# The last two chunks of a local attention and MoE kernel as one pair: GEMM1 with seven block products for eight

## The chip, the core and the metric

The kernel runs on one core of one Trainium2 chip. The metric is the device time of one execution in microseconds (us). A core has TensorE (PE, the matmuls), VectorE (DVE), ScalarE (ACT), GpSimd (POOL) and SyncE (SP, which issues the DMAs); they run side by side and wait for each other by semaphores. PE writes to eight PSUM banks of 128 x 512 floats; DVE and ACT read them.

## The reference

Attention makes x (4608 tokens x 512); a gated two-layer network follows, and it fills most of the time:

```python
out_up  = softmax attention on q, k, v averaged over 4 rows, repeated 4 times
out_local = softmax attention within |i - j| < 4
x = (out_up + out_local).transpose(0, 2, 1, 3).reshape(4608, 512)

def _moe_ref(x, w_in, w_out):          # w_in 512 x 2048, w_out 2048 x 512
    h = x @ w_in                       # GEMM1
    relu6 = np.clip(h + 3.0, 0.0, 6.0)
    g = h * relu6 / 6.0
    return (g @ w_out)                 # GEMM2
```

## The kernel before

**Precision.** Every operand of the two GEMMs is held as two fp32r parts: the rounded value (high) and what it leaves out (low). A product is three matmuls: high x high, high x low, low x high. For W_in these parts are the tiles `win[f]` (128 x 2 x 512; f is one of 16 blocks of 128 hidden columns, named wp in the trace), for W_out `wout[f]`; both stay in SBUF from the first chunk on.

**Chunks.** The 4608 tokens are nine chunks of 512 (0 to 8). For a chunk `plan_split` (line 958) makes the parts of x in the one buffer `rounded` (ACT or DVE the high part, L120 or L122; DVE or POOL the low part, L969), which is free when the chunk before has been through GEMM1. `plan_moe` (line 1050) then does for each f: `gemm1` (L1067), 12 matmuls into PSUM bank h0 or h1 (4 slices of 128 rows of W_in x 3 terms); `relu` on ACT (L1073); `gate` on DVE (L1077), which frees the bank; `hi` on ACT (L1081) and `lo` on DVE or POOL (L1085), the parts of g. `gemm2` (L1125) adds 12 matmuls per f into four banks o0 to o3, four groups of 128 tokens with 3 each. After the last f `plan_store` evicts each of the four (L1015 on ACT or L1017 on DVE, from few `ob` buffers) and SP stores it (L1021; for the last chunk L1032, L1034, L1038).

**Attention.** Its units for batches 1 to 7 lie among the chunks; batch 7, the last, is done during chunk 6. A unit loads q, k, v (L323, L397 to L411), writes its weights to DRAM and reads them back (L608, L635; L616, L643), transposes on DVE (L329, L631, L650), has short bursts on PE and ends with an addition on DVE (L757).

**What sets the order.** Every step is an `op` with an engine or a choice of engines, a cost, inputs, buffers to take and to free, and a due time. `emit` (line 1413) plays through these costs and writes each engine's instructions in the order that results; on the chip every engine keeps to its row. GEMM1 and GEMM2 come out as pairs: 24 matmuls of GEMM1 for two f, 24 of GEMM2 for two earlier f. SP's row is the queue for nearly all DMAs, loads and stores together; at most eight are under way, each waiting for the one eight before it.

## Time and profile before

| | |
|---|---|
| time, median of 3 runs | 917.17 us (916.25 to 917.22) |
| span of the profiled execution (the only time the page gives for it) | 912.1 us |
| PE busy | 895.3 us, 98% |
| DVE / ACT / POOL busy | 532.1 us, 58% / 448.9 us, 49% / 216.9 us, 24% |
| GEMM2, L1125, 1728 matmuls | 413.7 us busy, mean 392 ns of one |
| GEMM1, L1067, 1728 matmuls | 406.2 us busy, mean 390 ns of one |
| DMA | 93.49 MB, mean 102 GB/s |
| chain that ended last | PE 91% of the span, DMA 3%, DVE 2% |

The span runs from the first to the last instruction; launch and end lie outside it. Matmuls overlap, so the mean of one is longer than the step from one to the next. Whether an engine that waits costs anything is read from PE's row: where PE has no gap, it does not.

### The profile page before, as it was taken

The page shows a single profiled execution, that of the slowest core. Times are in us where ns is not written, and L with a number is a line of the kernel's source. Part 1 is how long each engine was busy: PE and PEld are TensorE (multiplying, and loading weights), DVE is VectorE, ACT ScalarE, POOL GpSimd, SP SyncE. Part 2 cuts the span into 40 slices and gives each one's busy share as a digit, 9 for nine tenths or more (in the row PEclk, how much of TensorE's full clock was granted, in tenths as well). Part 3 has the DMA queues.
Part 4 walks back from the last instruction along what each step waited for, and adds up shares of the span by engine and source line. Part 5 has one row for each costly group of instructions (what it writes and reads, how often), then busy time and mean ns, then how long its engine had stood idle before and what let it go on. Part 6 is the DMA issues. An engine that isn't in the chain of part 4 may idle for free.

```text
span 912.1 us, 19238 instructions
## 1 busy us (share of the span) xinstructions
PE 895.3 (98%) x7009; PEld 732.2 (80%) x7009; DVE 532.1 (58%) x978; ACT 448.9 (49%) x1465; POOL 216.9 (24%) x301
## 2 busy tenths in 40 slices
PE   7999999999999999999999999999999999999997
PEld 5667788788888888888888888888888888888886
DVE  7898876576766766656665666665553332233222
ACT  5898866465555555454655545454542222232221
POOL 3655542144522141123212331223000000000000
PEclk9999999999999999999999999999999999999999
DMA  8999843366657644755365536554531010001001
GB/s 227 252 234 247 198 127 72 93 117 124 134 120 142 142 94 114 141 104 106 72 130 109 111 82 140 104 105 92 121 80 22 0 47 1 1 1 46 1 1 46
DMA packets 312302, 93.49 MB, mean 102 GB/s; under 512 B 251408, under 2 KB 297616, under 8 KB 312208
## 3 DMA queue, kind: packets, MB, share of 16 engines
q1 hardware_dynamic: 310928, 90.51, 45.2%
q10 hardware_dynamic: 1280, 1.76, 0.6%
q8 instruction: 55, 0.90, 0.4%
q14 instruction: 39, 0.32, 0.1%
HBM read 69.60 MB, written 22.61 MB: 101 GB/s over the span
## 4 chain that ended last, share of the span: by engine, by line
PE 91%; DMA 3%; DVE 2%; ACT 1%; SPq 1%; POOL 1%; issue 1%; ACTq 0%; DVEq 0%; POOLq 0%
PE o L1125 43%; PE h L1067 41%; PE a L709 2%; PE h L752 2%; PE a L501 1%; PE h L664 1%; DMA early<-in_v_dram 1%; DMA out_dram<-arena 1%; DMA arena<-in_k_dram 1%; DMA arena<-in_q_dram 0%; PE h L501 0%; POOL early L582 0%; DVE first L757 0%; SPq L1021 0%; SPq L291 0%
## 5 line engine op out<-in xcount | busy, mean ns | idle before, releaser
L1125 PE MATMUL o<-wp,rounded 128*128 128x512 f32 x1728 | 413.7, 392 | 2.2 <-DVE arena L1017 1.1
L1067 PE MATMUL h<-rounded,wp 128*128 128x512 f32 x1728 | 406.2, 390 | 1.0 <-DVE arena L1077 1.0
L1067 PEld LDWEIGHTS h<-rounded,wp 128*128 128x128 f32 x1728 | 323.5, 188 | 69.2 <-DVE arena L1077 1.4
L1125 PEld LDWEIGHTS o<-wp,rounded 128*128 128x128 f32 x1728 | 321.5, 188 | 71.5 <-DVE arena L1017 1.6
L1077 DVE SCALAR_TENSOR_TENSOR arena<-arena,h 128x512 f32<-128x512 f32 x144 | 98.1, 682 | 144.4 <-ACT arena L1073 143.9
L1073 ACT ACTIVATE arena<-h 128x512 f32<-128x512 f32 x144 | 85.9, 596 | 183.4 <-PE h L1067 180.2
L1085 DVE TENSOR_TENSOR rounded<-arena,rounded 128x512 fp32r<-128x512 f32 x114 | 81.8, 719 | 131.1 <-PE o L1125 114.2
L1081 ACT CAST rounded<-arena 128x512 fp32r<-128x512 f32 x144 | 89.0, 618 | 110.6 <-PE o L1125 72.8
L1085 POOL TENSOR_TENSOR rounded<-arena,rounded 128x512 fp32r<-128x512 f32 x30 | 39.9, 1329 | 191.7 <-PE o L1125 173.0
L565 ACT ACTIVATE arena<-arena 128x64 f32<-128x64 f32 x240 | 80.3, 338 | 0.5
L422 POOL TENSOR_TENSOR arena<-arena 32x256 f32<-32x256 f32 (+1 forms) x26 | 22.5, 866 | 113.0 <-DMA arena<-in_v_dram 99.8
L329 DVE STREAM_TRANSPOSE arena<-arena 128x576 f32<-128x576 f32 x56 | 43.2, 771 | 9.9 <-DMA arena<-in_k_dram 5.0
L378 POOL TENSOR_TENSOR arena<-arena 128x144 f32<-128x144 f32 x33 | 14.9, 452 | 128.7 <-DMA arena<-in_v_dram 45.4
L565 ACT ACTIVATION_READ_ACCUMULATOR arena<-arena 128x1 f32 x240 | 45.5, 190 | 0.0
L684 ACT ACTIVATE arena<-h 128x144 f32<-128x144 f32 x24 | 7.0, 291 | 67.1 <-PE h L664 67.1
L380 POOL TENSOR_TENSOR arena<-arena 128x144 f32<-128x144 f32 x66 | 38.7, 587 | 5.2
L541 ACT ACTIVATE arena<-arena 128x1 f32<-128x1 f32 (+1 forms) x78 | 15.0, 193 | 43.2 <-DVE arena L554 43.2
L420 DVE TENSOR_REDUCE arena<-arena 128x128 f32<-128x512 f32 (+1 forms) x26 | 27.5, 1062 | 12.7 <-PE h L664 10.4
L582 DVE TENSOR_TENSOR arena<-arena 128x640 f32<-128x640 f32 (+1 forms) x41 | 33.8, 827 | 1.2
L423 POOL TENSOR_TENSOR arena<-arena 32x128 f32<-32x128 f32 (+1 forms) x26 | 13.6, 523 | 73.5 <-PE h L664 52.7
L709 PE MATMUL a<-arena 64*64 64x64 f32 x1200 | 28.8, 225 | 0.0
L202 POOL TENSOR_TENSOR wp<-early,wp 128x1024 fp32r<-128x1024 f32 (+1 forms) x10 | 23.4, 2349 | 17.8 <-ACT wp L198 17.8
(184 smaller groups left out, 766.5 us busy)
## 6 DMA issues: line engine op xcount, KB each, us to landing
rawp<-in_w_in_dram SPq DMA_DIRECT2D x16, 512.0 KB
rawp<-in_w_out_dram SPq DMA_DIRECT2D x16, 512.0 KB
arena<-in_q_dram SPq DMA_DIRECT2D x112, 72.0 KB
arena<-in_k_dram SPq DMA_DIRECT2D x112, 72.0 KB
pl<-arena SPq DMA_DIRECT2D x24, 320.0 KB
arena<-pl SPq DMA_DIRECT2D x96, 80.0 KB
arena<-in_v_dram SPq DMA_DIRECT2D x28, 256.0 KB
out_dram<-arena SPq DMA_DIRECT2D x89, 72.0 KB
```

The costliest lines, as they stand in the source:

```text
L329: nc.vector.transpose(out=qk[kind], in_=qk[kind])
L380: eng.tensor_tensor(t, t, x[:, :, r], op=ALU.add)
L420: eng.tensor_reduce(out=vd, in_=raw.rearrange("p r e -> p e r"), op=ALU.add, axis=AX.X)
L565: nc.scalar.activation(x[:, j], x[:, j], AF.Exp, bias=m[:, j:j + 1], scale=0.125, accum_out=s[:, j:j + 1])
L582: eng.tensor_tensor(x, x, s.unsqueeze(2).broadcast_to(list(x.shape)), op=ALU.mult)
L709: nc.tensor.matmul(st["ps", g][half:half + WIN, jj * D:jj * D + WIN], qk_of("q")[hs, k_first:k_first + WIN], qk_of("k")[hs, k_first:k_firs ...
L1067: nc.tensor.matmul(st["ps"], win[f][:, wt, kk * P:(kk + 1) * P], xs[part][:, kk], start=(kk == 0 and i == 0), stop=(kk == NK - 1 and i == ...
L1073: nc.scalar.activation(st["t"], st["ps"], AF.Relu, bias=3.0)
L1077: nc.vector.scalar_tensor_tensor(out=t, in0=t, scalar=6.0, in1=st["ps"], op0=ALU.min, op1=ALU.mult)
L1081: nc.scalar.copy(st["gh"], st["t"])
L1085: eng.tensor_tensor(st["gl"], st["t"], st["gh"].bitcast(F32), op=ALU.subtract)
L1125: nc.tensor.matmul(otile[n, m], gt[:, ms], wout[f][:, wt], start=(f == 0 and i == 0), stop=(f == NF - 1 and i == 2),)
```

## The change

Chunks 7 and 8 are planned together by a new function, `plan_strassen`, in place of `plan_split` and `plan_moe`. Let x have the blocks b11, b21 (chunk 7, upper and lower 256 of the 512 model rows) and b12, b22 (chunk 8). A group i takes two blocks of hidden columns, f = 2i and 2i + 1, so W_in gives four blocks of 256 x 128, and GEMM1 for the group is a product of 2 x 2 blocks: eight products of 6 matmuls each (2 slices x 3 terms). Strassen's identity in Winograd's form makes it seven, from sums of blocks:

- of x, once (`combine`, L1263, and `split`, L120, L122, L1241): t1 = b12 - b11, t2 = b22 - t1, t3 = b22 - b12, t4 = b21 - t2. With b11, b21 and b22 these are seven operands, each with high and low part. Two lie in `rounded` (t1, b22), the other five in the tiles win[6] to win[15] as soon as chunk 6 has read them.
- of W_in, in each group: `whole` (L1333) adds high and low, `mix` (L1340) makes four sums of 128 x 256, `s_hi` (L1354, ACT) and `s_lo` (L1357) their parts, in win[4] and win[5].

The seven products (L1370): p1, p6, p7, p5 go one after the other into one bank, the chain; ACT copies the bank after p1, p6 and p7 (`take_copy`, L1386: copies a, b, c). p2, p4, p3 have a bank each. DVE puts together c11 = p2 + a, less = c - b, c21 = p4 + c (all `plus_bank`, L1403, but `less`, L1406), last_u = chain - less (L1409), c12 = p3 + last_u; c22 is the chain itself. Then relu (L1413) and gate (L1417) as before: g11, g21 for chunk 7, g12, g22 for chunk 8. GEMM2 (L1460) of chunk 7 lies among the products of the next group; GEMM2 of chunk 8 follows when all eight groups are done, into the banks of the products, from gates kept in 16 buffers (`ts`). `plan_gemm2` makes the parts of g (L1442 on ACT, L1446 on DVE or POOL).

Since win[4] to win[15] are overwritten, `plan_spill` writes them to DRAM (L1178, 12 tiles) once chunk 5 is planned, and groups 2 to 7 read them back (L1321) into win[0] to win[3], two tiles for a group, while the groups before them run.

The diff, cut to its core:

```diff
+    def plan_spill(f):
+        to = spilled[f] = {}
+        def put_w():
+            to["d"] = dram.tile([P, 2 * 512], F32, name=f"wd{f}", tag=f"wd{f}")
+            nc.sync.dma_start(to["d"], win[f].bitcast(F32).rearrange("p i n -> p (i n)"))
+        to["op"] = op("SP", 0.5, put_w, [read_w[f]], size=dma(P, 4096), dl=start_of(PAIR0 - 1))
...
+        NAMES = {"b11": 6, "b21": 8, "t2": 10, "t3": 12, "t4": 14, "t1": 16, "b22": 18}
...
+        split("b11", None, [], [], 0, 0)
+        split("b21", None, [], [], 0, 1)
+        t1 = combine("t1", of_x(1, 0), of_x(0, 0), lambda o, c: ready_x(1, 0, o, c) + ready_x(0, 0, o, c), cuts(0, 1))
+        t2 = combine("t2", of_x(1, 1), of_tmp("t1"), lambda o, c: t1 + ready_x(1, 1, o, c), cuts(1))
+        split("t2", lambda: tmp("t2"), t2, [])
+        t3 = combine("t3", of_x(1, 1), of_x(1, 0), lambda o, c: ready_x(1, 1, o, c) + ready_x(1, 0, o, c), cuts(1))
+        split("t3", lambda: tmp("t3"), t3, ["t3"])
+        t4 = combine("t4", of_x(0, 1), of_tmp("t2"), lambda o, c: t2 + ready_x(0, 1, o, c), cuts(0))
+        split("t4", lambda: tmp("t4"), t4, ["t4"])
+        split("t1", lambda: tmp("t1"), t1, ["t1"])
+        split("b22", None, [], [], 1, 1)
...
+        def blocks(i):
+            return win[2 * (i % 2)] if i > 1 else win[2 * i], win[2 * (i % 2) + 1] if i > 1 else win[2 * i + 1]
...
+        def weight(i, j, part, kk):
+            first, second = blocks(i)
+            ks = slice(kk * P, (kk + 1) * P)
+            if j in (1, 2):
+                return first[:, part, (j - 1) * half * P:][:, ks]
...
+        MOVING = {1: "b11", 2: "b21", 3: "b22", 4: "t4", 5: "t1", 6: "t2", 7: "t3"}
...
+            if i > 1:
+                def load(x):
+                    nc.sync.dma_start(blocks(i)[x].bitcast(F32).rearrange("p i n -> p (i n)"), spilled[2 * i + x]["d"])
+                ld = [op("SP", 0.5, partial(load, x), [spilled[2 * i + x]["op"]] + loaded[i - 2], size=dma(P, 4096))
+                      for x in range(2)]
...
+            def whole(x, eng):
+                if x == 0:
+                    st["w"] = buf("wf", i, [P, 2, 512])
+                w = blocks(i)[x].bitcast(F32)
+                eng.tensor_tensor(st["w"][:, x], w[:, 0], w[:, 1], op=ALU.add)
...
+                out_, x, y, o = ((a22, a21, a22, ALU.add), (a21, a11, a21, ALU.subtract),
+                                 (a11, a22, a11, ALU.subtract), (a12, a12, a11, ALU.subtract))[k]
...
+            for a in range(2):
+                o = op("ACT", 0.6, partial(s_hi, a), [mixes[2 + a], mixes[1]] + (s_free[i - 1, a] if i else deps))
+                s_done[a] = op(on("lo", 512), 0, partial(s_lo, a), [o], free=[("wf", i)], lock=True)
...
+            def product(j, key, first, last):
+                if ("bank", i, key) not in places:
+                    places["bank", i, key] = bank("hp", (i, key))
+                ps = places["bank", i, key]
+                for kk in range(half):
+                    for x, (wt, part) in enumerate(((0, 0), (0, 1), (1, 0))):
+                        nc.tensor.matmul(
+                            ps, weight(i, j, wt, kk), xpart(MOVING[j], part)[:, kk], start=first and kk == 0 and x == 0,
+                            stop=kk == half - 1 and x == 2, skip_group_check=True)
...
+            p1 = mul(1, "chain", 0.0)
+            p2 = mul(2, "p2", 1.36)
+            ca = op("ACT", 0.6, partial(take_copy, "a"), [p1], take=[tcs["a"]])
+            p6 = mul(6, "chain", 4.08, [ca], False)
+            cb = op("ACT", 0.6, partial(take_copy, "b"), [p6], take=[tcs["b"]])
+            p7 = mul(7, "chain", 6.8, [cb], False)
+            cc = op("ACT", 0.6, partial(take_copy, "c"), [p7], take=[tcs["c"]])
+            p4 = mul(4, "p4", 8.16)
+            p5 = mul(5, "chain", 10.2, [cc], False)
+            p3 = mul(3, "p3", 12.24)
...
+            def plus_bank(name, key):
+                nc.vector.tensor_tensor(st[name], places["bank", i, key], st[name], op=ALU.add)
...
+            def less(eng):
+                eng.tensor_tensor(st["b"], st["c"], st["b"], op=ALU.subtract)
...
+            def last_u():
+                nc.vector.tensor_tensor(st["b"], chain(), st["b"], op=ALU.subtract)
...
+            c11 = op("DVE", 0.7, partial(plus_bank, "a", "p2"), [p2, ca, p6], free=[("hp", (i, "p2"))])
+            d = op(on("s512", 1), 0, less, [cc, cb], lock=True)
+            c21 = op("DVE", 0.7, partial(plus_bank, "c", "p4"), [p4, cc, d], free=[("hp", (i, "p4"))])
+            e = op("DVE", 0.7, last_u, [p5, d])
+            c12 = op("DVE", 0.7, partial(plus_bank, "b", "p3"), [p3, e], free=[("hp", (i, "p3"))])
...
+        NG = NF // 2
+        for i in range(NG):
+            plan_group(i)
+            if i:
+                at = t0 + GROUP * i
+                for x, pos in enumerate(((2.72, 3.4, 5.44, 6.12), (9.5, 11.56, 13.6, 14.28))):
+                    plan_gemm2(0, 2 * (i - 1) + x, [at + p for p in pos])
...
+        if n == PAIR0:
+            plan_strassen(n, prev_last)
+            break
         plan_split(n, prev_last)
         prev_last = plan_moe(n)
+        if n == SPILL_AT:
+            for f in range(4, NF):
+                plan_spill(f)
...
+PAIR0, SPILL_AT, GROUP = 7, 5, 15.0
...
+    "s512": {"POOL": (1.35, 0.0), "DVE": (0.72, 0.0)},
+    "s256": {"POOL": (0.75, 0.0), "DVE": (0.4, 0.0)},
...
+        "hp": ["h0", "h1", "a0", "a1"], "q0": ["a0"], "q1": ["a1"], "q2": ["h0"], "q3": ["h1"],
+        "tc": [(x, TOK * 4) for x in range(slots["qk"][0][0] + 4096, slots["qk"][0][0] + 4096 + 4 * 2048, 2048)],
+        "wf": [(slots["qk"][0][0], 4096)],
+        "xT": [(slots["qk"][0][0] + 4096 * (1 + i), 4096) for i in range(4)],
+        "ts": [(slots["qk"][0][0] + 2048 * (6 + i), 2048) for i in range(5)] + slots["raw"]
+        + [(x + i * 2048, 2048) for x in (xb0, xb1) for i in range(4)] + [(slots["qk"][0][0], 2048)],
...
```

**PE's row where the pair begins** (o0 to o3 are chunk 6's GEMM2 banks; h0, h1, a0, a1 the banks of GEMM1 and of the products; wp0_556 is win[0], wp1_668 win[1], wp8_968 and wp10_971 the tiles that hold b11). Before:

```order
L1125 MATMUL o2_7605<-wp29_1696,rounded_66 128x512 x3
L1125 MATMUL o3_7611<-wp29_1696,rounded_66 128x512 x3
L1067 MATMUL h0_8205<-rounded_66,wp0_556 128x512 x12
L1067 MATMUL h1_8219<-rounded_66,wp1_668 128x512 x12
L1125 MATMUL o0_7592<-wp30_1743,rounded_66 128x512 x3
L1125 MATMUL o1_7600<-wp30_1743,rounded_66 128x512 x3
L1125 MATMUL o2_7605<-wp30_1743,rounded_66 128x512 x3
L1125 MATMUL o3_7611<-wp30_1743,rounded_66 128x512 x3
```

After:

```order
L1126 MATMUL o2_7629<-wp29_1696,rounded_66 128x512 x3
L1126 MATMUL o3_7635<-wp29_1696,rounded_66 128x512 x3
L1370 MATMUL a1_8256<-wp8_968,wp0_556 128x512
L1370 MATMUL a1_8256<-wp10_971,wp0_556 128x512
L1370 MATMUL a1_8256<-wp8_968,wp0_556 128x512 x2
L1370 MATMUL a1_8256<-wp10_971,wp0_556 128x512
L1370 MATMUL a1_8256<-wp8_968,wp0_556 128x512
L1126 MATMUL o0_7616<-wp30_1743,rounded_66 128x512 x3
L1126 MATMUL o1_7624<-wp30_1743,rounded_66 128x512 x3
L1126 MATMUL o2_7629<-wp30_1743,rounded_66 128x512 x3
L1126 MATMUL o3_7635<-wp30_1743,rounded_66 128x512 x3
L1126 MATMUL o0_7616<-wp31_1746,rounded_66 128x512 x3
```

In place of 24 matmuls of chunk 7's first two f stands product 1 of the first group (6 matmuls), and chunk 6's last GEMM2 follows at once; the other six products of that group come after it without GEMM2 between them.

**DVE's row over the same time and on into the second group.** Before, it is gates, low parts and chunk 6's evictions:

```order
L1077 SCALAR_TENSOR_TENSOR arena_65<-arena_65,h0_8205 128x512
L1077 SCALAR_TENSOR_TENSOR arena_65<-arena_65,h1_8219 128x512
L1085 TENSOR_TENSOR rounded_66<-arena_65,rounded_66 128x512
L1017 TENSOR_SCALAR arena_65<-o0_7592 128x512
L1017 TENSOR_SCALAR arena_65<-o1_7600 128x512
L1085 TENSOR_TENSOR rounded_66<-arena_65,rounded_66 128x512
L1017 TENSOR_SCALAR arena_65<-o2_7605 128x512
L1077 SCALAR_TENSOR_TENSOR arena_65<-arena_65,h0_8269 128x512
L1017 TENSOR_SCALAR arena_65<-o3_7611 128x512
```

After (a0_8300, a1_8256, h0_8318, h1_8342 are product 2, the chain, products 4 and 3 of the first group; wp6_879 holds the low parts of the weight sums):

```order
L1403 TENSOR_TENSOR arena_65<-a0_8300,arena_65 128x512
L1417 SCALAR_TENSOR_TENSOR arena_65<-arena_65 128x512
L1406 TENSOR_TENSOR arena_65<-arena_65 128x512
L1446 TENSOR_TENSOR rounded_66<-arena_65,rounded_66 128x512
L1357 TENSOR_TENSOR wp6_879<-arena_65,wp4_937 128x512
L1403 TENSOR_TENSOR arena_65<-h0_8318,arena_65 128x512
L1409 TENSOR_TENSOR arena_65<-a1_8256,arena_65 128x512
L1417 SCALAR_TENSOR_TENSOR arena_65<-arena_65,a1_8256 128x512
L1417 SCALAR_TENSOR_TENSOR arena_65<-arena_65 128x512
L1403 TENSOR_TENSOR arena_65<-h1_8342,arena_65 128x512
L1446 TENSOR_TENSOR rounded_66<-arena_65,rounded_66 128x512
L1333 TENSOR_TENSOR arena_65<-wp1_668 128x512
```

Here c11, a gate, `less` and a low part of g come first, then the low half of the second group's weight sums (L1357), and only behind it c21 of the first group, which frees bank h0; last_u, two gates and c12 follow.

**SP's row in chunk 5's time**, as a piece of the difference (wd is the DRAM copy of a W_in tile, pl and pd hold attention weights):

```order
 L406 DMA arena<-in_v_dram 128x512
 L411 DMA arena<-in_v_dram 16x512 x2
+L1178 DMA wd_6816<-wp_937 128x1024
+L1178 DMA wd_6819<-wp_879 128x1024
+L1178 DMA wd_6821<-wp_968 128x1024
+L1178 DMA wd_6823<-wp_971 128x1024
 L397 DMA arena<-in_v_dram 64x5x128
 L643 DMA arena<-pl_3_6795 32x20x32 x4
```

The first four tiles stand ahead of a unit's loads; four, two, one and one more follow at later places.

## Rows read from the trace of the kernel before

**Rows 1.** Busy time by stretch: us, PE busy (matmuls), PEclk, DMA share, GB/s.

```profile
640.00:900.00 260.00, 260.00 (x1337) 1.00 0.11 27
```

**Rows 2.** Timeline, PE: start us, us, engine, line, operation, out<-in, count.

```profile
721.88 5.60 PE L1125 MATMUL o<-wp,rounded 128*128 128x512 f32 x24
727.33 5.60 PE L1067 MATMUL h<-rounded,wp 128*128 128x512 f32 x24
...
895.96 11.09 PE L1125 MATMUL o<-wp,rounded 128*128 128x512 f32 x48
```

**Rows 3.** Timeline from 738 us, PE, ACT and DVE (in brackets: idle before).

```profile
738.21 5.60 PE L1067 MATMUL h<-rounded,wp 128*128 128x512 f32 x24
...
741.17 0.60 ACT L1073 ACTIVATE arena<-h 128x512 f32<-128x512 f32 x1 [5.09 <-PE h L1067]
741.80 0.69 DVE L1077 SCALAR_TENSOR_TENSOR arena<-arena,h 128x512 f32<-128x512 f32 x1 [0.97 <-ACT arena L1073]
```

**Rows 4.** Groups by shape, 560 to 912 us: busy us, mean ns, idle before.

```profile
L1077 DVE SCALAR_TENSOR_TENSOR arena<-arena,h 128x512 f32<-128x512 f32 x60 | 41.1, 685 | 97.4 <-ACT arena L1073 97.4
L1085 DVE TENSOR_TENSOR rounded<-arena,rounded 128x512 fp32r<-128x512 f32 x56 | 38.9, 694 | 83.4 <-PE o L1125 77.1 <-ACT rounded L1081 5.0 <-PE h L1067 1.3
L969 DVE TENSOR_TENSOR rounded<-arena,rounded 128x1024 fp32r<-128x1024 f32 x2 | 2.5, 1225 | 1.3 <-ACT rounded L120 1.3
L1034 DVE TENSOR_SCALAR arena<-o 128x256 f32<-128x256 f32 x4 | 1.7, 425 | 4.4 <-ACT arena L1032 2.5 <-DMA out_dram<-arena 1.8
L1073 ACT ACTIVATE arena<-h 128x512 f32<-128x512 f32 x60 | 35.9, 599 | 128.0 <-PE h L1067 127.5
```

**Rows 5.** Timeline of chunk 6, PE and DVE.

```profile
687.76 11.04 PE L1067 MATMUL h<-rounded,wp 128*128 128x512 f32 x48
...
694.09 0.69 DVE L1077 SCALAR_TENSOR_TENSOR arena<-arena,h 128x512 f32<-128x512 f32 x1 [0.66 <-ACT arena L1073]
...
703.52 0.82 DVE L757 TENSOR_TENSOR arena<-h,arena 128x288 f32<-128x288 f32 x2
```

**Rows 6.** Busy time by stretch, DVE.

```profile
684.00:722.00 38.00, 13.11 (x25) 1.00 0.07 14
```

**Rows 7.** Timeline around the first spill's place: SP, then DVE, then PE.

```profile
578.43 0.95 SPq L411 DMA_DIRECT2D arena<-in_v_dram  x2
585.46 0.62 SPq L397 DMA_DIRECT2D arena<-in_v_dram  x1
...
593.14 0.65 DVE L1077 SCALAR_TENSOR_TENSOR arena<-arena,h 128x512 f32<-128x512 f32 x1
...
597.45 5.60 PE L1067 MATMUL h<-rounded,wp 128*128 128x512 f32 x24
```

**Rows 8.** Stretches, SP: length, clock, DMA share, GB/s.

```profile
580.00:584.00 4.00, 1.00 0.19 67
600.00:604.00 4.00, 1.00 0.94 223
```

**Rows 9.** The loads of the weights at the start: such a stretch; timeline, SP and ACT.

```profile
40.00:44.00 4.00, 1.00 1.01 393
...
117.30 1.39 SPq L169 DMA_DIRECT2D rawp<-in_w_out_dram  x3
...
124.48 0.68 ACT L180 ACTIVATE rawp<-rawp 128x512 f32<-128x512 f32 x1
```

**Rows 10.** Timeline, DVE and POOL: one addition alone, one beside POOL's.

```profile
598.91 0.83 DVE L582 TENSOR_TENSOR arena<-arena 128x640 f32<-128x640 f32 x1
...
619.21 1.29 POOL L1085 TENSOR_TENSOR rounded<-arena,rounded 128x512 fp32r<-128x512 f32 x1 [4.41 <-PE o L1125]
...
619.92 1.26 DVE L582 TENSOR_TENSOR arena<-arena 128x640 f32<-128x640 f32 x1
```

**Rows 11.** Timeline of chunk 6's stores, SP and DVE.

```profile
737.08 7.54 SPq L1021 DMA_DIRECT2D out_dram<-arena  x17
...
740.14 0.69 DVE L1017 TENSOR_SCALAR arena<-o 128x512 f32<-128x512 f32 x1 [0.97 <-DMA out_dram<-arena]
```

More of the change, by code (lines that the diff above doesn't have):

```diff
@@ L991, in tile_local_down_attention_moe @@
     last_split = {}
-    otile, st_o, gemms, firsts, first_half = {}, {}, [], {}, {}
+    otile, st_o, gemms, firsts, first_half, read_w = {}, {}, [], {}, {}, {}
     def stores(t, cnt):
@@ L1106, in plan_moe @@
             a = steps[-1]
+            read_w[f] = a
             first_half[n, f] = steps[:-1] if width == NK // 2 else []
@@ L1172, in busy @@
+    spilled = {}
     def busy(n):
@@ L1269 @@
     "ob": {"ACT": (0.6, 0.0), "DVE": (0.64, 0.0)},
+    "s512": {"POOL": (1.35, 0.0), "DVE": (0.72, 0.0)},
+    "s256": {"POOL": (0.75, 0.0), "DVE": (0.4, 0.0)},
 }
 PEN = {"lo": {"DVE": 0.0}, "pool4": {"POOL": 0.0}, "ev": {"DVE": 5.0}, "sum4": {"POOL": -10.0},
-    "norm": {"DVE": 5.0}, "normd": {"DVE": 5.0, "ACT": 5.0}, "minus": {"DVE": 5.0}, "xhi": {"DVE": 1.0}, "xlo": {"POOL": 2.0}, "gl": {"POOL": 10.0}, "ob": {"DVE": 5.0}}
+    "norm": {"DVE": 5.0}, "normd": {"DVE": 5.0, "ACT": 5.0}, "minus": {"DVE": 5.0}, "xhi": {"DVE": 1.0}, "xlo": {"POOL": 2.0}, "s512": {"DVE": 5.0}, "s256": {"DVE": 5.0}, "gl": {"POOL": 10.0}, "ob": {"DVE": 5.0}}
 def _slots():
```

190 lines of the change are left out of this document (added).

## The prediction

> **What bounds the kernel now.** I read the busy table by stretches first: from 640 to 900 us TensorE (PE) is busy in every microsecond at a granted clock of 1.00 [rows 1]. From 727.33, where chunk 7 begins, PE does blocks of 24 matmuls in turn, GEMM1 and GEMM2, each starting where the last one stopped [rows 2]. Only a removed matmul, or one that streams faster, shortens this stretch; the other engines matter only if the change makes one late. The pace: from 727.33 to 895.96 lie 744 matmuls (768 of chunks 7 and 8, 24 of chunk 6's GEMM2, less the last 48), so 168.63 / 744 = 0.2267 us each [rows 2].
>
> **Matmuls removed.** GEMM1 of the two chunks is 2 x 16 blocks of 12 matmuls, 384. Now it is 8 groups of 7 products of 6, 336. GEMM2 stays at 384. So 48 x 0.2267 = **-10.88 us**, all on the path. Shape, three terms (high x high, high x low, low x high) and a weight load for each matmul are unchanged, so I take the same pace. The Trainium skill ("TensorE: Matmul & The Clock Gate", "Wait — 56ns, not 53.3ns?") gives a warm matmul of 512 columns 215.7 ns from start to start; the 744 matmuls here took 226.7 each, so row and page differ, and the measurement decides. By the page's figure the gain would be 48 x 0.2157 = 10.35 and the result 907.2 us.
>
> **Copies inside the chain.** Products 1, 6, 7, 5 accumulate in one PSUM bank, and ScalarE (ACT) copies it after 1, 6 and 7. In the block that starts at 738.21 the first 12 matmuls end at 740.93; ACT starts 0.24 later, takes 0.60, and the vector engine (DVE) starts 0.03 after that [rows 3]. The way back from ACT to PE is not shown; between 0.03 and 0.24 it makes a copy 0.87 to 1.08 us. The shortest cover PE has between a product and the next of its chain is 6 matmuls, 1.36 us. So 0, with 0.28 to 0.49 to spare, as long as ACT stands ready. If one other ACT operation of 0.60 comes first, the chain loses 0.11 to 0.32 each time.
>
> **Vector work of a group.** A full group is 42 + 24 matmuls, 66 x 0.2267 = 14.96 us. DVE gets 18 operations in it: 15 over 512 columns (0.69 each, between 685 and 694 ns) and 3 over 256 (0.42), 11.6 us; ACT 11 of about 0.6, 6.7 us [rows 4]. I followed the third group's rows in order with these durations and hops, from product 1 at 0. The ends: c11 (p1 + p2, waits for p6) 6.4, gate g11 7.9, its low part 9.3, less 10.0, first low half of the next weight sums 10.7, c21 11.4, last_u (waits for p5) 12.5, gates g22 13.2 and g21 13.9, c12 14.65, second low half 15.35, low part of g21 16.1, the two sums `whole` of the next weights 17.5, gate g12 18.2, three `mix` 19.5; the next c11 starts at 20.7. What PE wants of it comes early: c21 frees p4's bank for the next group's p2 (16.3) 4.9 us ahead, the low half ending at 10.7 is for the next p6 (19.0). So 0 on the path, but DVE's row has only 1.2 us over in a group.
>
> **The first group.** It has no GEMM2 of its own to fill it. PE runs p1 727.33 to 728.69, chunk 6's last 24 GEMM2 matmuls to 734.13, then p2, p6, p4, p7, p3, p5 to 742.29. On DVE the sum that frees p4's bank stands behind the low half of the second group's weight sums. That one follows an ACT copy that must wait for p5: 742.29 + 0.24 + 0.60 + 0.03 + 0.69 = 743.85, and then the sum, to 744.55. The second group's p2, which takes this bank, would start at 742.29 + 1.36 + 0.68 = 744.33. With a hop of 0.03 to 0.24 PE stops for 0.25 to 0.46 us: **+0.4**. It happens once; later groups have those 4.9 us.
>
> **Making the operands.** Two chunk splits (4096 columns high, 4096 low) become seven operands (7168 and 7168) and four differences (4096). At 1.23 us per 1024 columns [rows 4] DVE and GpSimd get some 8.6 us more, ACT up to 3.1. Most of it lies on DVE between 684 and 722, where 38 us hold 13.1 of work [rows 6]; by the order some 13 us come in. The last attention result is there at 703.5 [rows 5], the first product that needs it (p6) starts at 735.5. The narrowest place is chunk 6's four GEMM1 blocks from 687.76: the gate of the second starts at 694.09 [rows 5], and now a low part of 896 columns (1.09) stands ahead of it that must wait until the block is read at 693.20 + 0.24. The gate then ends at 695.22, the fourth block wants its bank at 687.76 + 36 x 0.2267 = 695.92. So 0, with 0.5 to 0.7 left.
>
> **Spilling and reloading W_in.** Twelve tiles of 512 KB go to DRAM on SP's queue, 4, 4, 2, 1, 1 at a time. The first four stand between the loads that SP issued up to 579.4 and the one at 585.46 [rows 7], where the DMA engines are 19% busy [rows 8]; behind them wait the loads of the last attention units, and in the end a transpose on DVE, a gate and PE. Price of a tile: at 223 GB/s (small packets, share 0.94) 2.35 us [rows 8], at 393 GB/s in the weight loads 1.33 [rows 9]. Four are 5.3 to 9.4 us, of which 6 find idle engines: 0 to 3.4 late. A gate there began at 593.14, took 0.65, and its bank was next wanted at 597.45 [rows 7], so it may slip by 3.4 to 3.6. I take 0, nearer to the emptier row; a gain is excluded because PE has no idle time there to give back. The reloads: a tile may be fetched when the last product on it has ended (9.5 in its group) and DVE adds it up at 16.1. Three weight tiles issued at 117.30 were in use at 124.48 [rows 9], so at most 7.2 us, 17.2 at worst, and DVE has nothing urgent until 20.7. So 0.
>
> **Evictions behind stores.** Chunk 6's last eviction now stands on ACT ahead of the first group's third copy, and it waits until the store of the second one has landed, since the two share a buffer. Before, SP needed 0.44 us for each of the stores' 17 issues, and DVE went on with the third eviction 1.3 us after the four issues of the first, at 740.14 [rows 11]. Now the first two evictions can start at 732.4 on DVE and SP can issue from 733.2 on: nine issues and 1.3 us, 738.5. The eviction may start as late as 739.5 before the copy behind it makes p5 late. So 0, with 1.0 us left; a store that lands later costs what it exceeds that, once. In the pair's end chunk 7's evictions wait the same way, but there ACT makes two of chunk 8's GEMM2 inputs between one eviction and the next, and PE takes 2.72 us for each.
>
> **End.** Chunk 8's GEMM2 follows as 192 matmuls with all inputs made; the last evictions and stores stand as before: 0.
>
> **Sum.** The span is 912.1; the page gives no other time for the profiled execution, and the median of the runs, 917.17, is 5.1 above it (launch and end, untouched). Span 912.1 - 10.88 + 0.4 = 901.6, and 917.17 - 10.5 = **906.7 us**.
>
> **Rivals.** (a) *Hand-overs that leak in every group.* If an ACT operation gets ahead of two copies in each of eight groups, 16 x 0.32 = 5.1 us: 911.8. For it: the 0.28 spare. Against: the order puts the copies first in ACT's row. (b) *Slower: DVE's row becomes the cycle.* If DVE waits out each ACT step instead of filling it (four gates 0.87 each, one copy 0.87, two weight halves 0.63), 11.6 + 3.5 + 0.9 + 1.3 = 17.3 us a group, and eight groups give 8 x (17.3 - 14.96) = 18.7: 925.0. It decides from 14.96 + 10.88 / 8 = 16.3 us a group. For it: only 1.2 us are over, and a GpSimd addition blocks DVE (0.83 alone, 1.26 while GpSimd's lasted [rows 10]); one GpSimd addition a group costs 0.4 or so. Against: other work lies in most of those waits. The Trainium skill ("SBUF — State Buffer", "SBUF: two separate sides") has this as a lock held for a whole instruction, against operations with two SBUF inputs; the row agrees. (c) *Spill or reload exposed.* One burst of four fully on the path, 5.3 to 9.4: 912 to 916. (d) *Products don't keep the pace.* The gain is gone at 0.2267 x 768 / 720 = 0.242 us each, 917. Against: GEMM1 and GEMM2, with operands from different buffers, both run at 5.44 us per 24 [rows 2].
>
> **How the numbers follow.** Forecast, 905.3 to 908.5: 0.68. (a) 908.5 to 911.8: 0.14. (c) 0.05, (d) 0.04, (b) 0.09. The lower end is the gain without any stop, 906.3, less the spread of the runs (0.97); the upper one is (a)'s full price; 0.82 lies inside. 0.2% (1.8 us) is about what a measurement of this kernel can tell from no change. Faster: forecast, (a) and (c), 0.87. Same: 0.04, (d). Slower: 0.09, (b).
>
> **What would show it.** Right: PE busy without a break up to 744 us; one stop of about 0.4 near 744.3, before product 2 of the second group; 24 matmuls in 5.44 us in the groups too; the last matmul, which now ends at 895.96 + 48 x 0.2267 = 906.8, some 10.5 us earlier; a span near 901.6. Wrong: PE idle before product 7 or 5 behind an ACT copy (a); DVE above 90% busy and PE waiting for it in every group (b); gates between 590 and 700 us held up by a transpose that waits for its DMA (c); 24 matmuls in more than 5.5 us without a wait (d). The forecast as a whole falls if PE's idle time in the pair is above 2 us.

## The result

The changed kernel took 903.84 us (median; 900.67 to 904.18) against 916.71 us before, in which a further run of 913.01 stands beside the three that were known. The ratio is 0.9872 [0.9843, 0.9902]. The forecast was 906.7 us, 10.5 less than 917.17, with a range of 905.3 to 911.8: the direction and the size of the step were right, and the time fell below the range.

The span of the profiled execution went from 912.1 to 902.0 us; 901.6 was forecast. The page's first part shows fewer matmuls and busier vector engines:

```profile
PE 883.8 (98%) x6961; PEld 722.2 (80%) x6961; DVE 592.2 (66%) x1073; ACT 472.5 (52%) x1511; POOL 237.5 (26%) x316
```

PE in the pair, from its first matmul to the end of its last (us, PE busy with the count, granted clock, DMA share, GB/s), first before, then after:

```profile
727.33:907.05 179.72, 179.72 (x793) 1.00 0.05 14
```

```profile
727.87:896.67 168.80, 168.80 (x745) 1.00 0.17 53
```

The stretch is 10.92 us shorter, with 48 matmuls fewer (counted the same way), and PE is busy in all of it at a granted clock of 1.00. The remaining difference of the two spans lies outside: the pair begins 0.54 later, and after the last matmul 5.33 us follow in place of 5.05. -10.92 + 0.54 + 0.28 = -10.1.

Timeline of PE where the pair begins, the place of [rows 2] (start, us, engine, line, operation, out<-in, count):

```profile
727.87 1.52 PE L1370 MATMUL a<-wp,wp 128*128 128x512 f32 x6
729.23 5.60 PE L1126 MATMUL o<-wp,rounded 128*128 128x512 f32 x24
734.67 2.88 PE L1370 MATMUL a<-wp,wp 128*128 128x512 f32 x12
...
741.47 1.52 PE L1370 MATMUL a<-rounded,wp 128*128 128x512 f32 x6
742.83 1.52 PE L1370 MATMUL a<-wp,wp 128*128 128x512 f32 x6
744.19 0.84 PE L1460 MATMUL o<-wp,rounded 128*128 128x512 f32 x3
744.87 1.52 PE L1370 MATMUL h<-wp,wp 128*128 128x512 f32 x6
```

Every line starts where the last one's matmuls are through; none has idle time in brackets. Product 1 of the second group starts at 742.83, its product 2, the one for which a stop was forecast, at 744.87, right behind three GEMM2 matmuls. So the mechanism is as forecast, less one stop. What has to be explained is the level: why 903.8 and not 906.7.

### The profile page after: what moved, and what is told of

The parts are those of the page before. It is cut to its first block, busy times and chain, and to the rows that moved or that the text cites. A ratio compares the mean times of both kernels' runs of the same rounds, so it can differ in the third digit from the quotient of the medians.

```text
span 902.0 us, 19402 instructions
## 1 busy us (share of the span) xinstructions
PE 883.8 (98%) x6961; PEld 722.2 (80%) x6961; DVE 592.2 (66%) x1073; ACT 472.5 (52%) x1511; POOL 237.5 (26%) x316
## 4 chain that ended last, share of the span: by engine, by line
PE 90%; DMA 3%; DVE 2%; SPq 2%; ACT 1%; issue 0%; POOL 0%; ACTq 0%; DVEq 0%
PE o L1126 33%; PE h L1067 31%; PE o L1460 5%; PE a L1370 5%; PE h L1370 4%; PE a L1460 2%; PE h L1460 2%; PE a L709 2%; PE h L752 2%; PE a L501 1%; PE h L664 1%; DMA early<-in_v_dram 1%; DMA arena<-in_k_dram 1%; DMA out_dram<-arena 1%; SPq L323 0%; DMA arena<-in_q_dram 0%
## 5 line engine op out<-in xcount | busy, mean ns | idle before, releaser
L1126 PE MATMUL o<-wp,rounded 128*128 128x512 f32 x1344 | 324.1, 393 | 2.7 <-DVE arena L1017 1.6
L1067 PE MATMUL h<-rounded,wp 128*128 128x512 f32 x1344 | 316.9, 390 | 1.2 <-DVE arena L1077 1.0
L1067 PEld LDWEIGHTS h<-rounded,wp 128*128 128x128 f32 x1344 | 251.3, 188 | 54.8 <-DVE arena L1077 1.4
L1126 PEld LDWEIGHTS o<-wp,rounded 128*128 128x128 f32 x1344 | 249.5, 188 | 56.8 <-DVE arena L1017 2.0
L1077 DVE SCALAR_TENSOR_TENSOR arena<-arena,h 128x512 f32<-128x512 f32 x112 | 76.0, 679 | 61.8 <-ACT arena L1073 61.3
L1073 ACT ACTIVATE arena<-h 128x512 f32<-128x512 f32 x112 | 66.6, 594 | 78.8 <-PE h L1067 76.2
L1081 ACT CAST rounded<-arena 128x512 fp32r<-128x512 f32 x112 | 68.9, 615 | 73.9 <-PE o L1126 44.1
L1085 POOL TENSOR_TENSOR rounded<-arena,rounded 128x512 fp32r<-128x512 f32 x27 | 35.9, 1331 | 63.9 <-PE o L1126 45.1
L1460 PE MATMUL o<-wp,rounded 128*128 128x512 f32 x192 | 49.2, 389 | 0.0
L1460 PEld LDWEIGHTS o<-wp,rounded 128*128 128x128 f32 x192 | 36.0, 188 | 7.5
L1370 PE MATMUL a<-wp,wp 128*128 128x512 f32 x150 | 37.2, 389 | 0.0
L1446 DVE TENSOR_TENSOR rounded<-arena,rounded 128x512 fp32r<-128x512 f32 x27 | 18.6, 690 | 26.8 <-PE h L1460 21.1
L420 DVE TENSOR_REDUCE arena<-arena 128x128 f32<-128x512 f32 (+1 forms) x26 | 27.6, 1065 | 12.9 <-PE h L664 10.8
```

The source lines that it names most:

```text
L420: eng.tensor_reduce(out=vd, in_=raw.rearrange("p r e -> p e r"), op=ALU.add, axis=AX.X)
L1067: nc.tensor.matmul(st["ps"], win[f][:, wt, kk * P:(kk + 1) * P], xs[part][:, kk], start=(kk == 0 and i == 0), stop=(kk == NK - 1 and i == ...
L1073: nc.scalar.activation(st["t"], st["ps"], AF.Relu, bias=3.0)
L1077: nc.vector.scalar_tensor_tensor(out=t, in0=t, scalar=6.0, in1=st["ps"], op0=ALU.min, op1=ALU.mult)
L1081: nc.scalar.copy(st["gh"], st["t"])
L1085: eng.tensor_tensor(st["gl"], st["t"], st["gh"].bitcast(F32), op=ALU.subtract)
```

## The experiments

**What they tell apart.** Theory: the change takes 48 matmuls off PE's row and costs next to nothing else, and the forecast failed because its starting level was not that of the profiled execution. Rival: the change gives back 2 to 3 us more somewhere, outside the pair or outside the span. Beside that, two rooms on which the forecast rested (the copy in the chain, DVE's row) were measured by filling them. The table has all runs; "pair" is chunks 7 and 8 on PE from first start to last end in the profile; "time less span" is the time of an execution less the span of the same execution (median of the runs).

| kernel | us, median (lowest to highest) | ratio to before | pair starts | pair lasts | time less span |
|---|---|---|---|---|---|
| before, profiled | | | 727.33 | 179.72 | |
| after, profiled | 903.84 (900.67 to 904.18) | 0.9872 [0.9843, 0.9902] | 727.87 | 168.80 | 2.16 |
| before_again | 913.25 (911.97 to 916.13) | 0.9999 [0.9987, 1.0012] | 726.50 | 179.70 | 1.78 |
| after_again | 904.11 (901.95 to 905.68) | 0.9890 [0.9873, 0.9907] | 729.55 | 168.83 | 2.18 |
| after_third | 904.27 (900.63 to 906.66) | 0.9881 [0.9854, 0.9907] | 728.74 | 168.84 | 2.15 |
| eighth_product | 912.95 (911.60 to 915.61) | 0.9998 [0.9985, 1.0011] | 726.03 | 179.71 | 2.17 |
| small_spill | 901.70 (900.65 to 904.90) | 0.9871 [0.9851, 0.9890] | 725.80 | 168.80 | 2.2 |
| spill_only | 913.30 | | 726.60 | 179.70 | 1.8 |
| dve_two | 902.33 | | 725.82 | 169.74 | 1.8 |
| dve_four | 908.89 | | 724.67 | 177.42 | 1.8 |
| dve_eight | 936.09 | | 726.46 | 202.95 | 1.8 |
| copy_b_twice | 903.07 | | 725.07 | 171.01 | 2.2 |
| copy_b_thrice | 911.00 | | 728.60 | 175.29 | 2.2 |

The kernel before had 913.05 us (911.64 to 916.72) beside before_again, after_again, eighth_product and small_spill, and 914.55 (911.42 to 917.06) beside after_third, dve_four, dve_eight and copy_b_thrice; beside spill_only, dve_two and copy_b_twice it ran once, 914.10. The kernels without a range ran once; what they tell is read from their profiles.

**The kernel before against itself.**

> The kernel before, unchanged, timed against itself. Theory: the change is worth 10.3 to 10.9 us, and the prediction missed because it set the profiled execution (span 912.1) equal to the median of other runs (917.17). In the four runs of the kernel after, time less span is 2.1 to 2.2 each; so the profiled execution of before took about 914.3, not 917.2. Then here too time less span is 2.1 to 2.2 in every run, and single runs of the same program lie 3 to 4 us apart. Rival: before has about 5 us outside its span and after 2, so that the change itself gave 2.9 us back there: time less span near 5 in the runs of this kernel. Ratio 1.000 within 0.002 by either.

Time less span is 1.75 to 1.86 us in all runs of this kernel in these sets, not 5, and not the 2.1 to 2.2 that I expected either. The time of the execution that the profile shows is not on record; with 1.8 outside its span it took about 912.1 + 1.8 = 913.9 us (an estimate). The 917.17 to which the forecast's saving was applied is the median of runs that took some 3.3 us longer than that; no trace of them exists. Runs of this one program lie between 911.4 and 917.1 in these sets. The rival, 5 us outside the span of before, is not borne out.

**The changed kernel again.**

> The changed kernel, unchanged, with more runs. Theory: 10.3 to 10.9 us faster than before (ratio 0.9881 to 0.9888), time less span 2.1 to 2.2; the pair of chunks again 168.8 us from its first matmul to its last, and what differs between two profiles of it lies before 330 us, in the start. Rival (the gain is larger than the matmuls taken out): 12.9 us or more, ratio 0.986 or below, with a difference before the pair that every run shows.

> The changed kernel again, on whatever chip this falls on. Theory: the pair 168.8 us from its first matmul to its last, 10.9 less than before; the end 0.3 longer and 0.37 more outside the span (2.15 against 1.78 us), so 10.2 us faster with the same start: ratio 0.9888, 0.9875 to 0.990. Rival (the changed program starts later by 1 to 2 us in every execution): ratio 0.990 to 0.991, and the pair begins at 728 to 730 us again, where before and the eight-product kernel begin it at 725.8 to 727.3.

The pair lasts 168.83 and 168.84 us. Ratios of 0.9890 and 0.9881 against 913.05 and 914.55 are 10.0 and 10.9 us; the first comparison gives 0.0128 x 916.71 = 11.7. All three intervals hold the forecast's 10.5 (ratio 0.9885), though after_again's ratio lies just outside the 0.9881 to 0.9888 expected of it; the rival of 12.9 us or more (ratio 0.986) is outside after_again's interval. The rival of after_third, a later start, is not settled. Its sign was seen: the pair began at 729.55 and 728.74. In the seven other kernels that hold the pair, whose source up to there is the same but for the size of small_spill's writes, it began at 724.67 to 728.60, so the planned work ahead of the pair does not explain it; but whether the built program starts later by 1 to 2 us as a rule, or by chance in three profiles, these runs do not tell.

Where this scatter of 4.9 us arises can be read from the start. Stretch from 20 to 32 us (us, granted clock, DMA share, GB/s) and the first GEMM2 matmuls of chunk 0, in before_again, then in after_again:

```profile
20.00:32.00 12.00, 1.00 1.05 207
```

```profile
57.27 3.73 PE L1125 MATMUL o<-wp,rounded 128*128 128x512 f32 x15 [1.08 <-DVE wp L202]
```

```profile
20.00:32.00 12.00, 0.72 0.94 196
```

```profile
22.31 0.58 PE L435 MATMUL a<-early,four 64*16 64x128 f32 x2 [1.23 <-DMA early<-in_v_dram]
...
60.99 3.72 PE L1126 MATMUL o<-wp,rounded 128*128 128x512 f32 x15 [1.06 <-DVE wp L202]
```

At this matmul the thirteen profiles already lie between 57.27 and 61.19 us. In the three that pass it at 59.8 to 60.0 (before, after, after_third) the DMA engines moved 181 to 185 GB/s in that stretch; in the six at 57.3 to 58.3 they moved 200 to 207 GB/s at full clock; in the three at 59.3, 61.0 and 61.2 the granted clock was 0.86, 0.72 and 0.72 there. One (spill_only, 59.15 with 207 at full clock) does not fit, and nothing was varied to test it: the two go together in twelve of thirteen profiles, and a cause is not shown. Further differences are a wait of 0.8 to 2.0 us at 170 to 174 us in all of them, and one of 0.2 to 1.6 between 298 and 321 in four. From 330 us to the pair no profile shows a wait of PE.

**Eight products again.**

```diff
-                for kk in range(half):
+                for kk in [k for _ in range(2 if j == 3 else 1) for k in range(half)]:
```

> Product 3 of each group is computed twice into its bank, so GEMM1 has eight products for eight again, 48 matmuls more than the changed kernel, all else as it is. Theory: 48 x 0.2267 = 10.9 us slower than the changed kernel, so within 1 us of the kernel before; PE without a stop in the pair. Rival (hidden gain or loss elsewhere in the change): it differs from before by 2 us or more; at 2.4 us faster than before the surplus of the measured gain lies outside the matmuls.

```profile
726.03:905.74 179.71, 179.71 (x793) 1.00 0.16 49
```

With the 48 matmuls put back the pair takes 179.71 us, as long as before's 179.72, and the time is before's (ratio 0.9998). All the staging, the copies, the sums and the DRAM traffic are still in it. So the gain in the pair is the matmuls and nothing else, and the rest costs nothing there that shows. The expected 10.9 to the changed kernel is 10.91 by the pair; by the medians it is 8.8. The profile of after_again starts the pair 3.5 us later than this one (729.55 against 726.03); how far that holds for its other runs, of which there is no trace, is open.

**The spill and the reload.** In small_spill the transfers carry 16 of 1024 columns; spill_only is the kernel before with the twelve writes.

```diff
-            nc.sync.dma_start(to["d"], win[f].bitcast(F32).rearrange("p i n -> p (i n)"))
+            nc.sync.dma_start(to["d"][:, :16], win[f].bitcast(F32).rearrange("p i n -> p (i n)")[:, :16])
...
-                    nc.sync.dma_start(blocks(i)[x].bitcast(F32).rearrange("p i n -> p (i n)"), spilled[2 * i + x]["d"])
+                    nc.sync.dma_start(blocks(i)[x].bitcast(F32).rearrange("p i n -> p (i n)")[:, :16], spilled[2 * i + x]["d"][:, :16])
```

```diff
-        if n == PAIR0:
-            plan_strassen(n, prev_last)
-            break
```

> The 12 tiles of W_in written to DRAM and the 12 read back carry 16 of 1024 columns each; every DMA, its place in SP's row and its waits stay, so groups 2 to 7 run on the weights of the first two (the output is not the reference's). Theory: the traffic is hidden, 0.0 within 0.5 us of the changed kernel. Rival (the spill or the reload is exposed, 1.33 to 2.35 us a tile): 5 to 9 us faster than the changed kernel.

> The kernel before with the twelve writes of W_in to DRAM after chunk 5 and nothing else of the change; nothing reads them. Theory: no wait of PE after 330 us, as in before; chunks 7 and 8 again 179.7 us from first to last matmul, so its own time changes by nothing that the start's scatter would let one see. Time less span tells where the 0.37 us outside the span come from: 2.15 if it is the twelve buffers in DRAM, 1.78 if it is the pair's code. Rival (the spill is exposed by 1.33 us or more a tile): waits of PE between 575 and 640 us.

```profile
725.80:894.60 168.80, 168.80 (x745) 1.00 0.06 16
```

```profile
726.60:906.30 179.70, 179.70 (x793) 1.00 0.05 14
```

The first row is small_spill, the second spill_only (us, PE busy, clock, DMA share, GB/s): with the traffic cut to 16/1024 the pair lasts 168.80 as with all of it, with the writes alone 179.70 as without; neither shows a wait of PE after 330 us. small_spill's median is 2.4 us under after_again's, more than the 0.5 expected, but its profile has that lead at 60 us (58.12 against 60.99), 500 us before the first spill. Price of the traffic on PE's row: 0. Time less span is 1.8 us with the twelve buffers, so they are not what adds 0.37 outside the span; as the dve kernels, which hold the whole pair, have 1.8 too, the pair isn't either. That cause stays open.

**DVE's row filled up.**

```diff
                 nc.vector.tensor_tensor(st[name], places["bank", i, key], st[name], op=ALU.add)
+                for _ in range(4 if name == "b" else 0):
+                    nc.vector.tensor_tensor(st["b"], st["b"], st["b"], op=ALU.max)
```

(2 and 8 in the others.)

> Two more operations over 128 x 512 behind c12, which change nothing in the result. With four of them, 2.79 us, a group took 16.22 us, so DVE's row and its waits for ACT alone make 16.22 - 2.79 = 13.4 us, 1.5 over; the prediction's row said 1.2 over. Two take 1.40. By the trace's 1.5: no stop from the third group on. By the prediction's 1.2: some 0.2 us a group, 1.4 to 3 us in all, with what a stop costs beside its idle time (0.3). In the second group both expect a stop of up to 0.3: there the stop was 1.68 with four.

> Behind the sum c12 of each group DVE does four more operations over 128 x 512, 0.60 to 0.69 us each, which change nothing in the result: 2.4 to 2.8 us a group. By the prediction's row (1.2 us over in a group, as waits for ACT can't be filled) the row falls behind by 1.2 to 1.6 us a group; some 4.9 us of lead are used up first, so after four groups PE stops, 4 to 8 us in all. Rival (all of DVE's idle time, 14.96 - 10.74 = 4.2 us a group, can be used): no stop of PE.

> The same with eight operations, 4.8 to 5.5 us a group. By the prediction's row 3.6 to 4.3 us a group are missing, eight groups 29 to 34, less the lead of 4.9: 24 to 29 us slower than the changed kernel. Rival (all idle time can be used): 0.6 to 1.3 a group, less the lead: 0 to 5 us.

The fourth group of the changed kernel by engine (us, then busy time of PE, PEld, DVE, ACT and POOL, clock, DMA share, GB/s), and dve_four's timeline: DVE with the added operations and its neighbours, ACT ahead of one stop, PE with the first stop and that of each of three groups:

```profile
772.75:787.71 14.96, 14.96 (x67) 12.39 (x66) 10.74 (x20) 6.40 (x12) 1.05 (x1) 1.00 0.21 70
```

```profile
789.18 0.68 DVE L1403 TENSOR_TENSOR arena<-h,arena 128x512 f32<-128x512 f32 x1
789.89 2.87 DVE L1405 TENSOR_TENSOR arena<-arena 128x512 f32<-128x512 f32 x4
792.68 0.69 DVE L1357 TENSOR_TENSOR wp<-arena,wp 128x512 fp32r<-128x512 f32 x1
...
783.56 0.62 ACT L1444 CAST rounded<-arena 128x512 fp32r<-128x512 f32 x1 [0.76 <-DVE arena L1419]
784.08 0.58 ACT L1386 COPY arena<-a 128x512 f32<-128x512 f32 x1
...
748.27 3.01 PE L1370 MATMUL a<-wp,wp 128*128 128x512 f32 x12 [1.68 <-ACT arena L1386]
...
768.49 1.66 PE L1370 MATMUL h<-rounded,wp 128*128 128x512 f32 x6 [0.56 <-ACT arena L1386]
...
784.71 1.66 PE L1370 MATMUL a<-rounded,wp 128*128 128x512 f32 x6 [0.55 <-ACT arena L1386]
...
800.93 1.65 PE L1370 MATMUL a<-rounded,wp 128*128 128x512 f32 x6 [0.55 <-ACT arena L1386]
```

DVE is idle for 14.96 - 10.74 = 4.2 us of a group, and yet four operations more make the group 784.71 - 768.49 = 16.22 us. They come 0.70 apart, 2.79 us, and from c12 to the operation behind them it is 792.68 - 789.18 = 3.50 us, where neighbours in DVE's row start 0.60 apart: so the row is 2.90 longer. The chain behind a stop: DVE ends a gate late, ACT's cast of it waits 0.76, copy c stands behind that cast in ACT's row, and product 5 waits for the copy. So the rival "all idle time can be used" falls, and the row's own length is 16.22 - 2.90 = 13.3 us: 1.6 to spare, where the prediction's walk had 1.2 (the 1.5 expected for dve_two reckoned with 2.79). dve_two lies between, with a row 1.46 longer: one shown stop of 0.23 in the second group, none after it, the pair 0.94 longer:

```profile
747.97 3.03 PE L1370 MATMUL a<-wp,wp 128*128 128x512 f32 x12 [0.23 <-ACT arena L1386]
```

My 4.9 us of lead for dve_four were wrong: the stop comes in the second group already (1.68 us), because ACT's copies stand behind ACT operations that wait for DVE; the pair is 8.6 longer, above the 4 to 8 expected. dve_eight is 34.2 longer, where 24 to 29 were expected; the difference has two parts, the missing lead and the clock. Four of its stops, timeline, and the stretches of the first:

```profile
769.71 2.93 PE L1370 MATMUL h<-wp,wp 128*128 128x512 f32 x6 [2.81 <-ACT arena L1386]
772.44 1.86 PE L1462 MATMUL o<-wp,rounded 128*128 128x512 f32 x6
...
789.35 2.26 PE L1370 MATMUL a<-wp,wp 128*128 128x512 f32 x6 [2.81 <-ACT arena L1386]
...
809.02 1.66 PE L1370 MATMUL a<-wp,wp 128*128 128x512 f32 x6 [2.81 <-ACT arena L1386]
...
828.15 2.93 PE L1370 MATMUL h<-wp,wp 128*128 128x512 f32 x6 [2.99 <-ACT arena L1386]
```

```profile
766.90:769.70 2.80, 0.01 (x1) 1.00 0.44 159
769.71:772.50 2.79, 2.79 (x7) 0.50 0.02 6
```

Where the clock fell behind a stop, the group up to the next took 789.35 - 769.71 = 19.64 us; where it stayed, 828.15 - 809.02 = 19.13. The second agrees with the row: eight operations make it 5.81 longer, and 13.3 + 5.8 = 19.1. The six groups from the stop that ends at 752.97 to the one that ends at 870.14 took 117.2, some 2.4 over six times 19.13, an estimate of the clock's part; the rest of the miss, 2.8 to 7.8, holds the lead of 4.9 that was not there.

**Copy b made more than once.**

```diff
-                nc.scalar.copy(st[name], chain())
+                for _ in range(3 if name == "b" else 1):
+                    nc.scalar.copy(st[name], chain())
```

(2 in the other.)

> ACT makes copy b (after product 6) three times into the same buffer. In the changed kernel such a copy starts at 778.45, ends at 779.04, and product 7, which needs it, starts at 779.55 with nothing in between. Two more at ACT's pace of 0.49 end at 780.02. With a hop of 0.03 to 0.24 from ACT to PE (the prediction's bounds) PE stops 0.50 to 0.71 us in each of eight groups, 4.0 to 5.7 us in all, and the stop shows the hop. Rival (the chain has more room than the trace shows, product 7 not being held by the copy): no stop.

> Copy b made twice, 0.62 us more on ACT, where three times stopped PE by 0.61 us of idle time a group and lengthened the group by 0.93. Theory: the room of copy b is 0.46 us (product 7 due 1.36 after product 6 ends, copy and hops 0.90), so PE is late by 0.16 a group; whether the group grows by 0.16 or by 0.3 to 0.5 tells whether the part of a stop beside the idle time is paid for a short stop too. Over seven groups 1.1 to 3.5 us. Rival (the room is over 0.62): no change of the group's 14.96.

Copy b in the changed kernel, PE and ACT, then in copy_b_thrice, with the stops of three groups:

```profile
776.83 1.52 PE L1370 MATMUL a<-wp,wp 128*128 128x512 f32 x6
778.19 1.52 PE L1460 MATMUL o<-wp,rounded 128*128 128x512 f32 x6
779.55 1.52 PE L1370 MATMUL a<-wp,wp 128*128 128x512 f32 x6
...
778.45 0.59 ACT L1386 COPY arena<-a 128x512 f32<-128x512 f32 x1 [3.49 <-PE a L1370]
```

```profile
750.13 1.83 ACT L1387 COPY arena<-a 128x512 f32<-128x512 f32 x3 [0.48 <-PE a L1370]
...
752.01 3.06 PE L1370 MATMUL a<-wp,wp 128*128 128x512 f32 x12 [0.61 <-ACT arena L1387]
...
767.91 1.66 PE L1370 MATMUL h<-wp,wp 128*128 128x512 f32 x6 [0.61 <-ACT arena L1387]
783.80 1.66 PE L1370 MATMUL a<-wp,wp 128*128 128x512 f32 x6 [0.61 <-ACT arena L1387]
```

The copies end at 751.96 and product 7 starts at 752.01: the hop from ACT to PE is 0.05 us. So in the changed kernel a copy takes 0.26 + 0.59 + 0.05 = 0.90 of the 1.36 us that cover it, 0.46 to spare. Two more took 1.24 (0.62 from copy to copy into the same buffer, where 0.49 lies between ACT operations on different ones), 0.78 more than the room. A group took 783.80 - 767.91 = 15.89, 0.93 over 14.96: of it 0.61 are shown idle, 0.16 are the modelled end of the last matmul before the stop, and 0.14 the six behind it, 1.66 for 1.52. Seven groups show such a stop, the eighth none: 6.5 in all, where 4.0 to 5.7 was expected for eight. The idle time shown lies within the 0.50 to 0.71 expected, but product 7 is late by 0.77, because the copies took 1.24 for 0.98, and what is lost behind the stop was not in the sum.

copy_b_twice, product 7 of the second and the third group:

```profile
747.22 3.06 PE L1370 MATMUL a<-wp,wp 128*128 128x512 f32 x12
...
762.50 1.67 PE L1370 MATMUL h<-wp,wp 128*128 128x512 f32 x6
```

No idle time is shown here, but the group takes 762.50 - 747.22 = 15.28 us, 0.32 over 14.96, and the pair 7 x 0.32 = 2.2 more. PE is late by 0.16, as expected, and pays the other 0.15 behind it.

## Why the prediction was right and wrong

**The step that failed: the level and the lower end.** The sum was made on the span, 912.1 - 10.5 = 901.6, and the span came out at 902.0. Then 10.5 was taken from 917.17, with the 5.1 us between the two put down to "launch and end, untouched". The runs show 1.8 us there (the term was mis-sized by 3.3); the other 3.3 is how far the median of the three recorded runs lay above the profiled execution, if 1.8 holds for that one too. Where those runs lost it no trace shows; in the profiles that exist, executions of one program differ in the start. From the execution's own level the same sum gives 912.1 + 1.8 - 10.5 = 903.4, and 903.84 was measured. The lower end of the range had the same flaw: it allowed 0.97 us for the scatter, the spread of three runs that happened to lie together, where the program's runs spread over 5.6 us. Nothing in the profile gave the 5.1; calling it launch was a guess.

**The removed matmuls: right.** -10.88 forecast, -10.92 in the pair, 10.91 when they were put back. The pace held: a full group of 66 matmuls takes 14.96 us, 0.2267 each, in the products as in GEMM2. The Trainium skill ("TensorE: Matmul & The Clock Gate", "Wait — 56ns, not 53.3ns?") has 215.7 ns for a warm matmul of 512 columns, by which, as an estimate, the pair would have gained 10.35; the trace does not agree with it here. Rival (d) is out.

**The stop in the first group: wrong, +0.4 forecast, 0 measured.** ACT and DVE of the changed kernel at that place:

```profile
741.32 0.62 ACT L1354 CAST wp<-arena 128x512 fp32r<-128x512 f32 x1
742.81 0.62 ACT L1354 CAST wp<-arena 128x512 fp32r<-128x512 f32 x1 [0.87 <-PE a L1370]
...
742.14 0.69 DVE L1357 TENSOR_TENSOR wp<-arena,wp 128x512 fp32r<-128x512 f32 x1
742.75 0.68 DVE L1403 TENSOR_TENSOR arena<-h,arena 128x512 f32<-128x512 f32 x1
```

The weight sums have two halves. The low half ahead of c21 in DVE's row follows the ACT copy at 741.32, which overwrites the half that products 6 and 7 had read, and waits for nothing; only the copy at 742.81 overwrites what product 5 reads and waits for it. I had given the second one's wait to the first. c21 ends at 743.43 and the bank is wanted at 744.87.

**The copies in the chain: right.** 0.28 to 0.49 to spare was forecast, 0.46 measured; with the hop of 0.05 the copy's 0.90 lies at the lower end of 0.87 to 1.08.

**The vector work of a group: right that it fits, the number near in part by luck.** 1.2 us over in DVE's row was forecast, 1.6 was found (16.22 less 2.90, and 19.13 less 5.81). Two errors of the walk offset each other: the operations come 0.60 apart where they follow each other, not 0.69, which makes its row some 1 us too long, and it had 2.2 us of waits where dve_four's row has 2.7. What was not seen is the way a late row reaches PE: through ACT's row and the copies, so that in dve_four and dve_eight rival (b) shows as rival (a), PE idle behind an ACT copy; copy_b_thrice brings on (a) without (b). Neither happened in the changed kernel, where DVE's row stays under 14.96. One row speaks for the lock that (b) named, a gate that took 1.62 us beside an addition of POOL, 0.69 elsewhere:

```profile
745.16 1.62 DVE L1417 SCALAR_TENSOR_TENSOR arena<-arena 128x512 f32<-128x512 f32 x1
...
744.94 1.29 POOL L1333 TENSOR_TENSOR arena<-wp 128x512 f32<-128x512 f32 x1
```

**Making the operands: right.** In the stretch of [rows 6] DVE now does 26.30 us of work for 13.11; some 13 us were forecast to come in. The narrow place, against [rows 5]:

```profile
688.31 11.04 PE L1067 MATMUL h<-rounded,wp 128*128 128x512 f32 x48
...
693.95 1.09 DVE L1241 TENSOR_TENSOR wp<-first,wp 128x896 fp32r<-128x896 f32 x1
694.96 0.68 DVE L1077 SCALAR_TENSOR_TENSOR arena<-arena,h 128x512 f32<-128x512 f32 x1
```

The low part stands ahead of the gate, which ends at 695.64; the bank is wanted at 688.31 + 8.16 = 696.47. PE's 48 matmuls run through, with 0.8 us left where 0.5 to 0.7 was forecast.

**Spill and reload: right, 0.** Against [rows 7], SP in the changed kernel:

```profile
579.94 2.54 SPq L1178 DMA_DIRECT2D wd<-wp  x4
586.01 0.62 SPq L397 DMA_DIRECT2D arena<-in_v_dram  x1
```

The load behind the four tiles is issued at 586.01 for 585.46, 0.55 later, and PE runs 0.54 later by then in any case: the tiles do not delay it. The gate of [rows 7] starts at 593.67 for 593.14, later by PE's shift too. The DMA engines moved 362 GB/s from 580 to 584 us, near the 393 of [rows 9] and far from the 223 of [rows 8], so the lower price was the right one. Rival (c) is out.

**Evictions behind stores and the end: right.** Copy c of the first group starts at 740.31, 0.20 after product 7 ends; ACT's two evictions of chunk 6, at 738.08 and 739.09, are done by then. After the last matmul 5.33, 5.12 and 5.12 us follow in the three profiles of the changed kernel, 5.05 and 5.30 in the two of before: no difference that stands out.

**The sum.** -10.9 in the pair, +0.37 outside the span, 0 elsewhere: -10.5. That the forecast's -10.5 is the same number is in part luck: it had the wrong +0.4 in the place of this 0.37, which it did not know. By whole times the three comparisons give 10.0 to 11.7, which neither confirms nor excludes the 0.37.

## What to carry to other kernels

Put the predicted difference on one execution's own time, and let the range take in how far single executions of the program lie apart: three runs close together say little about that, and the length of the changed stretch in the trace (here equal within 0.04 us from profile to profile) tells the effect of a change on that stretch far more sharply than the whole time. Where PE's row has no gap, removed matmuls times their pace is the gain, however much other work the change adds, as long as each engine's row with its own waits fits in the new cycle. Read that fit by walking the row, not from busy time: of DVE's 4.2 idle us a group only about 1.6 could be used.

## What the runs showed of the hardware

- A stop of PE costs about 0.3 us more than the idle time it shows: groups grew by 0.93 for 0.61 shown, and by 0.32 where the timeline showed none. Of the difference 0.16 is the modelled end of the last matmul ahead of the stop, and 0.14 to 0.15 is lost behind it.
- After some stops of 2.8 us the granted clock was 0.50, its lower level of 1.2 GHz, for the next 2.8 us (six matmuls in 2.93 us for 1.52), after another of the same length it was not (1.66). During the first of these stops itself the records show 1.00. In after_again it was at 0.50 from 22 to 28 us too, behind a wait of 1.23 us in a stretch where PE was half idle.
- The way from ACT to PE took 0.05 us, from PE to ACT 0.20 to 0.26.
- Time less span was 1.8 us in some programs and 2.15 in others, the same within 0.1 in all runs of a program but for a single one (eighth_product, 3.06); neither the DRAM buffers nor the pair's code decides it, and what does is open.
